# Fused attention and FFN on one core: the reciprocals' small transfers go from SyncE to ScalarE, the scheduler's prices for the partial sums are changed, and the whole order is drawn again

## The chip, the cores and the metric

The kernel runs on one core of one Trainium2 chip. Each core has five engines that run their own instruction streams in order: TensorE (PE; its weight loads are shown as PEld), VectorE (DVE), ScalarE (ACT), GpSimd (POOL) and SyncE (SP, which here issues transfers and computes nothing). An instruction waits at the head of its engine's stream until the semaphores it needs have come. The metric is the device time of the program in microseconds (us), less is better; of several runs the median is compared.

## The reference

```python
# q, k, v: (4, 12, 448, 64) float32; x: (4, 448, 768)
scores = scale * np.matmul(q, k.transpose(0, 1, 3, 2))      # causal mask, softmax over keys
scores = np.where(mask, -1000000000.0, scores)
scores = scores - np.max(scores, axis=-1, keepdims=True)
attn = np.exp(scores)
attn = attn / (np.sum(attn, axis=-1, keepdims=True) + 1e-09)
x = np.matmul(attn, v)                                       # heads side by side: d_model 768
...
mu = np.mean(x, axis=-1, keepdims=True)
var = np.mean((x - mu) ** 2, axis=-1, keepdims=True)
xn = (x - mu) / np.sqrt(var + 1e-06) * g_ln
ch = np.maximum(xn @ w_ch1, 0.0) @ w_ch2                     # 768 -> 3072 -> 768
return (x + ch).astype(np.float32)
```

Four batches, each an attention over twelve heads, then a layer norm and a two-layer network (FFN) with a residual.

## The kernel before

**The work.** The FFN is most of TensorE's stream. Every float32 operand is split into a high and a low part (`xh`, `xl`, `wh`, `wl`, `hh`, `hl`), and a product is three fast matmuls (high by high, high by low, low by high) of 128 x 128 weights and 448 columns. `ph` is a PSUM tile of the first layer (18 matmuls), `po` one of the second (36). These use three PSUM banks, tag `mm`. After a `ph`, ACT writes `hh` and DVE `hl`; after a `po`, DVE adds it to `xT`. The FFN of batches 0 and 1 runs in 96 slots `s` of 18 matmuls; the FFN of batches 2 and 3 runs at the end together (class `Pair`, tiles `bX`, `bY`, `bA`, with weights `wk` and `wp`).

**Attention** of a batch is done in six pairs of heads and is woven into the FFN before it: batch 1 beside batch 0's FFN, batches 2 and 3 beside batch 1's. `STARTS` gives the slot at which each pair is due. Batches 0 to 2 compute scores `sc` with queries on the partitions, exponentials `P`, normalise (`norm`), transpose on TensorE (`pt`) and multiply by `v` (`px`).

**Batch 3 has transposed scores** (`crossed`, `most`, `added`, `crossed_pv`): keys on the partitions, so nothing is transposed, but maximum and sum go across partitions. For each pair of heads:

1. TensorE writes the scores into two banks a head, one of tag `sc` and one of tag `pt` (two of each tag, so the next pair's scores need this pair's banks back).
2. DVE adds the mask (`bars`) and folds the blocks into `most`; POOL's `partition_all_reduce` gives the maximum `all`; DVE subtracts it (`P<-sc,all`, four instructions a head, the last readers of the banks); ACT takes the exponentials.
3. `added`: `sum` is made of one copy and three DVE additions of unequal width a head, POOL sums it over the partitions, and the row goes to DRAM (`turn`, one transfer a head), comes back as 64 x 14 (`r14`, shown as `r<-turn`), DVE adds 1e-9 and takes the reciprocal, it goes to DRAM again (`turnb<-r`) and comes back broadcast over 64 partitions (`over<-turnb`, one a head). Six small transfers a pair, 36 in all, all issued by SP, in line with all other loads and stores.
4. `crossed_pv`: TensorE multiplies `P` by `v` into `px` (a bank of tag `pv`, of which there is one), and DVE writes `xT = px * over`. A pair of heads that stands in `TWOT` is done with its neighbour: both `px` in a row, the second into a bank of tag `pt`.

After the sixth pair the mean `mb` is a matmul over the sum `acc` of the six `xT` (high and low part, `acch` and `accl`), then squares `xc`, the variance `var`, and its spread `rb`, which the inputs of `Pair` need (`xg`, and from them `xh`, `xl`, `xT1h`, `xT2h` and others).

**What sets the order.** The kernel records all instructions, and a scheduler in plain Python (`Plan.schedule`, `Plan.run`) orders them with a cost for each (`Plan.cost`: time on the engine, delay until others see the result, whether it shares a port), due times, and PSUM and SBUF buffers. The costs are in ns and are the planner's own, not measurements. `MOVES` shifts the due times of instructions picked by a pseudo-random draw: each entry has a seed, a size, a share, and a stretch. So any change of a cost, a slot or a seed gives another order on all engines.

Of the kernel before, what the change touches and what calls it, by code (L numbers as in the profile page):

```python
# [20 lines left out]
B, H, S, D = 4, 12, 448, 64  # L21
# [17 lines left out]
HOLE = [-7, 5]  # L39
EARLY = 44  # L40
GAP = 5
SECOND = 32000
BEHIND = 8400
EARLY_SLOT = 1450
SLACK, DMA_SLACK = 192, 5280
# [1 line left out]
IDLE, SLOWED = 2200, 4500  # L47
PASSES, PORT, LEAST, AFTER, URGENT, START = 6, 300, 300, 1500, 5000, 70000
MOVES = [
# [4 lines left out]
]  # L54
STEPS = 6
FIRST = -19
RAT0, TAT0, NAT0, END0, EV0 = [-2, 1, 3], [7, 8, 9, 10, 11], [6, 6], 13, [1, 1, 0, 1, 0]
BOTH, RAT = {1: [0, 1, 2, 3], 2: [5], 3: []}, [1, 0, 0]
SAT, TAT, NAT, END = [1, 0, 1, 0, 2], [4, 5, 5, 6, 6], [3, 3], 8
EV1, EV = [1, 1, 1, 1, 1], [1, 1, 0, 1, 0]  # L60
STARTS = {
    0: [-1, 6, 12, 17, 24, 30],
    1: [0, 5, 10, 14, 19, 24],
    2: [28, 32, 35, 39, 42, 46],
    3: [58, 61, 65, 68, 72, 75],
}
SPREAD1 = 43
PAIR = 84
KEEP0 = 36
TWOS = {}  # L70
VAR0, RB0, XC, XG = 1, 5, 3, 3
SPLIT, SENT, WIDE = (1, 2, 3), (), ('mb',)
COPIED = [6, 6, 4, 0]
AHEAD0 = 4
WARM, FILL, HOLD = 10, 29160, 3200
LATE = {"PR": 3500, "full": 6000, "qkraw": 6000, "vt": 3000, "kept": 2500, "scratch": 1500}
LEFT = {1: (0, 0), 2: (0, 1), 3: "S4", 4: (1, 1), 5: "S1", 6: "S2", 7: "S3"}
RIGHT = {1: "B11", 2: "B21", 3: "B22", 4: "T4", 5: "T1", 6: "T2", 7: "T3"}
ORDER1, ORDER2 = [1, 2, 6, 5, 7, 3, 4], [1, 5, 6, 3, 7, 2, 4]
KB, GX = KC // 2, 2  # L80
ELAG = [1, 4, 9]
BANKS = [("sc", 2), ("sc", 2), ("pt", 2), ("pt", 2), ("pv", 1), ("mm", 3), ("mm", 3), ("mm", 3)]
TURNED, OFFPOOL, LIBRARY, LAZY = {2: [], 3: [0, 1, 2, 3, 4, 5]}, (2, 3), 6300, 12000
KEYS = [(0, 0, 448), (128, 128, 320), (256, 256, 192), (320, 384, 64)]
SCT, SUMT, ENDT = 0, 4, 6
PB, VB, TWOT = 3, 1, {3: [0, 2, 4]}
NORMS = ['PPPPPP', 'EPPPPP', 'EEEEEE', 'EEEEEE']
NTMP, AHEAD = 6, 6
LAST = 239 / 256

# [115 lines left out]
class Plan:  # L206
# [99 lines left out]
    def cost(self, t):  # L306
        n, sbuf = t.size, [x for x in t.ins if x.buf.pool.space is None and x.idx.size > 8]
        psum = any(x.buf.pool.space == PSUM for x in t.ins)
        t.here = 0
        if t.engine == "sync":  # L310
            x = (t.outs + t.ins)[0]
            rate = 100 if n == P else 360 if x.p[1] - x.p[0] == P else 240 if x.p[1] - x.p[0] == D else 150 if n == 512 else 330
            cost = 650 if x.buf.name == "first_qk" else 60
            if x.buf.name.startswith("row"):
                return 60, 8000 * 320, False
            if any(y.buf.name.startswith("turn") for y in t.outs + t.ins):
                return 60, (500 if n < S else 100 if x.p[1] - x.p[0] == 1 else 640) * 320, False
            return cost, (x.p[1] - x.p[0]) * n * 4 * 320 / rate, False
        if t.engine == "tensor":
            if t.kw.get("rhs") is not None and t.kw["rhs"].dtype == BF16:  # L320
                return 0.84 * n, 220, False
            if t.method == "transpose":
                t.mode = "turned"
                return 97 if t.ins[0].dtype == F32 else 78, 220, False
            if t.kw["rhs"].dtype == F32R:
                return max(0.4175 * n + 2, 112), 220, False
            wide = t.outs[0].p[1] - t.outs[0].p[0] > D and t.kw["rhs"].p[1] - t.kw["rhs"].p[0] > D
            t.mode = "" if wide else "rows" if t.outs[0].p[1] > D + t.outs[0].p[0] else "columns"
            return (1.68 if wide else 0.84) * n + 5 if n > 1 else 195, 220, False
        if t.engine == "scalar":  # L330
            t.here = 100
            if t.kw.get("func") == ACTF.Exp:
                t.here = 10
                return 0.84 * n + 277, 70, False
            if isinstance(t.kw.get("scale"), View):
                return 0.835 * n + 188, 160, False
            more = 50 if not psum and t.ins[0].idx.flat[1] > t.ins[0].idx.flat[0] + 1 else 0
            return 0.835 * n + more + (66 if psum else 155 if "scale" in t.kw else 94), 160, False
        if t.engine == "gpsimd":
            t.here = 30  # L340
            if t.method == "memset":
                return 95 + 0.84 * n, 90, False
            if t.method == "tensor_scalar":
                return 240 + 0.835 * n, 90, True
            if t.method == "partition_all_reduce":
                t.mode = "library"
                return (1730 if t.kw["reduce_op"] == bass_isa.ReduceOp.max else 2970), 90, False
            return 2.5 * n + 60 if n > 8 else 1500, 90, bool(sbuf)
        t.here = 85
        if t.method == "bn_stats":  # L350
            n = t.ins[0].idx.size
        tiny = t.method == "tensor_scalar_add" and not psum and t.outs[0].buf.name != "r"
        fast = t.method in ("tensor_copy", "tensor_scalar") and not psum and n > 8
        more = 130 if n <= 8 or t.method == "tensor_scalar" and fast else 75
        if "accum_out" in t.kw:
            t.here = 150
        if n <= 8 and t.method in ("tensor_scalar_add", "reciprocal"):
            more = 68 if t.method == "tensor_scalar_add" else 96
        if t.method == "scalar_tensor_tensor" and isinstance(t.kw["scalar"], View):
            more = 128  # L360
        if t.method == "tensor_tensor" and t.outs[0].p[0]:
            more = 187
        return n / (1.92 if fast else 0.96) + more, t.here + 60, fast or tiny or (len(sbuf) > 1 and not psum)

    def schedule(self):
# [267 lines left out]
def kernel(ctx, tc, qk, v, w1, w2, g, out):  # L633
    nc = plan = Plan()
# [171 lines left out]
    class Att:  # L806
# [204 lines left out]
        def added(self, p):  # L1011
            V = nc.vector
            row = dr.tile([1, 2 * S], F32, name=f"turn{self.b}{p}")
            back = dr.tile([1, 2 * S], F32, name=f"turnb{self.b}{p}")
            for h in range(2):
# [5 lines left out]
                V.tensor_tensor(out=z[:, 3 * P:], in0=z[:, 3 * P:], in1=e[:, :D], op=ALU.add)  # L1021
                t = ap.tile([P, S], F32, tag="PT", name="all", bufs=8)
                nc.gpsimd.partition_all_reduce(t, z, channels=P, reduce_op=bass_isa.ReduceOp.add)
                nc.sync.dma_start(out=row[:, S * h:S * h + S], in_=t[:1, :])
            r = ap.tile([P, S], F32, tag="PT", name="r14", bufs=8)[:D, :14]
            flat = lambda t: t.rearrange("o (p x) -> (o p) x", p=D)
            nc.sync.dma_start(out=r, in_=row.turned(flat))
            V.tensor_scalar_add(r, r, 1e-9)
            V.reciprocal(r, r)
            nc.sync.dma_start(out=back.turned(flat), in_=r)  # L1030
            t = ap.tile([P, S], F32, tag=("y", "rb")[p % 2], name="over", bufs=1)
            for h in range(2):
                nc.sync.dma_start(
                    out=t[D * h:D * h + D, :], in_=back[:, S * h:S * h + S].turned(lambda t: t.broadcast_to([D, S])),
                )
            self.t["over", p] = t
# [835 lines left out]
```

## Time and profile before

| | before |
|---|---|
| median of 3 runs | 807.77 us (807.57 to 810.73) |
| profiled execution, its own time | 806.13 us |
| its span, first to last instruction | 804.2 us |
| TensorE busy | 782.8 us, 97% of the span |
| VectorE busy | 670.9 us, 83% |
| ScalarE busy | 488.0 us, 61% |
| GpSimd busy | 350.8 us, 44% |

The profile shows one execution. Busy time is an average over stages; what a change is worth is read from the stretch in which TensorE stands idle and from what ended the idle time. In a timeline row the bracket at the end is the idle time ahead of the row and what ended it.

### The profile page before, as it was taken

The numbers are of one execution on the slowest core, as the hardware profiler recorded it, in microseconds if no ns is written. First come the engines' busy times: TensorE is split into PE (matmuls) and PEld (weight loads), VectorE is DVE, ScalarE is ACT, GpSimd is POOL, SyncE is SP. The second block draws the span as 40 slices with busy tenths as digits, with TensorE's granted clock in tenths as the row PEclk, the third lists the DMA queues.
The fourth block names the chain that finished last, engine by engine and source line by source line (L and its number), as shares of the span: only waits on it lengthen the run. The fifth ranks groups of instructions, "written<-read, shape, count | busy, mean of one in ns | idle before, by whom it ended". The sixth has DMA issues, their size and how long they took to land. (4 is left out here: it accounts for less than half of the span.)

```text
span 804.2 us, 13502 instructions
## 1 busy us (share of the span) xinstructions
PE 782.8 (97%) x4434; PEld 711.8 (88%) x4434; DVE 670.9 (83%) x1396; ACT 488.0 (61%) x1046; POOL 350.8 (44%) x346
## 2 busy tenths in 40 slices
PE   9999999999999999998989799899999999999998
PEld 4679887898999878987969599899999999999997
DVE  6899987789989985899989659598888878878785
ACT  7999987889999963441343234574555546455461
POOL 4742024344162350255554018755545454464540
PEclk9999999999999999999999899999999999999999
DMA  9778897878888787754472687135244342533424
GB/s 230 266 245 298 311 330 271 303 270 276 286 288 306 235 255 247 255 167 130 135 224 79 226 304 243 56 111 164 74 126 139 88 149 63 158 99 112 123 90 167
DMA packets 69630, 158.80 MB, mean 197 GB/s; under 512 B 14989, under 2 KB 37785, under 8 KB 69561
## 3 DMA queue, kind: packets, MB, share of 16 engines
q1 hardware_dynamic: 69560, 157.95, 59.5%
q8 instruction: 35, 0.57, 0.3%
q14 instruction: 35, 0.28, 0.1%
HBM read 115.92 MB, written 39.99 MB: 194 GB/s over the span
## 5 line engine op out<-in xcount | busy, mean ns | idle before, releaser
L624 PE MATMUL ph<-xh,wh 128*128 128x450 f32 (+1 forms) x288 | 103.1, 363 | 2.2 <-ACT wh L624 2.1
L624 PE MATMUL ph<-xh,wl 128*128 128x450 f32 (+1 forms) x288 | 103.5, 364 | 0.0
L624 PE MATMUL po<-hh,wl 128*128 128x448 f32 x288 | 102.5, 360 | 0.0
L624 PE MATMUL po<-hl,wh 128*128 128x448 f32 x288 | 101.9, 359 | 0.0
L624 PE MATMUL po<-hh,wh 128*128 128x448 f32 x288 | 101.3, 358 | 0.0
L624 PE MATMUL ph<-xl,wh 128*128 128x450 f32 (+1 forms) x288 | 101.2, 357 | 0.0
L624 ACT ACTIVATE wp<-s 128x256 fp32r<-128x256 f32 (+1 forms) x114 | 51.6, 462 | 60.3 <-PE bY L624 15.9
L624 POOL TENSOR_TENSOR s<-u 128x256 f32<-128x256 f32 (+1 forms) x60 | 55.3, 939 | 64.4 <-DMA u<-scratch 50.3
L624 POOL TENSOR_SCALAR P<-P,r 112x336 f32<-112x336 f32 (+3 forms) x72 | 47.0, 671 | 64.6 <-DVE r L624 64.3
L624 ACT ACTIVATE wk<-u 128x256 fp32r<-128x256 f32 (+1 forms) x89 | 41.4, 466 | 52.5 <-PE bX L624 34.1
L624 ACT ACTIVATE P<-P,least 112x224 f32<-112x224 f32 (+3 forms) x128 | 67.2, 535 | 9.4 <-DVE least L624 9.4
L624 DVE TENSOR_TENSOR wp<-s,wp 128x256 fp32r<-128x256 f32 (+1 forms) x120 | 67.9, 577 | 1.6 <-ACT wp L624 1.2
L624 POOL TENSOR_TENSOR h<-b,h 128x448 fp32r<-128x448 f32 x36 | 43.4, 1207 | 53.5 <-ACT h L624 26.8
L624 DVE CUSTOM_DVE_ANT_0 P<-sc,mask 112x448 f32<-112x448 f32 (+3 forms) x128 | 51.9, 443 | 13.6 <-PE sc L624 12.0
L624 PEld LDWEIGHTS ph<-xh,wh 128*128 128x128 f32 x288 | 55.0, 191 | 4.3 <-ACT wh L624 2.6
L624 PEld LDWEIGHTS ph<-xh,wl 128*128 128x128 f32 x288 | 54.9, 191 | 2.5 <-issue 1.4
L624 PEld LDWEIGHTS po<-hh,wh 128*128 128x128 f32 x288 | 54.4, 189 | 2.1 <-issue 1.6
L624 PEld LDWEIGHTS po<-hl,wh 128*128 128x128 f32 x288 | 54.2, 189 | 2.1 <-issue 1.4
L624 PEld LDWEIGHTS ph<-xl,wh 128*128 128x128 f32 x288 | 55.0, 191 | 1.1 <-issue 0.7
L624 DVE TENSOR_TENSOR xT<-xT,bX 128x448 f32<-128x448 f32 (+1 forms) x73 | 44.6, 613 | 13.2 <-PE bX L624 13.1
L624 PEld LDWEIGHTS po<-hh,wl 128*128 128x128 f32 x288 | 54.3, 189 | 0.9 <-issue 0.5
L624 DVE TENSOR_TENSOR wl<-w,wh 128x768 fp32r<-128x768 f32 x48 | 48.8, 1018 | 3.1 <-ACT wh L624 2.8
(211 smaller groups left out, 2142.4 us busy)
## 6 DMA issues: line engine op xcount, KB each, us to landing
raw<-w_dram SPq DMA_DIRECT2D x39, 768.0 KB, 6.5
scratch<-w SPq DMA_DIRECT2D x48, 384.0 KB, 7.2
full<-scratch SPq DMA_DIRECT2D x24, 768.0 KB, 4.9
kept<-wl SPq DMA_DIRECT2D x30, 384.0 KB, 3.1
u<-scratch SPq DMA_DIRECT2D x24, 384.0 KB, 3.7
u<-scratch SPq DMA_DIRECT2D x36, 256.0 KB, 3.0
rawx<-w_dram SPq DMA_DIRECT2D x9, 768.0 KB
wk<-kept SPq DMA_DIRECT2D x36, 192.0 KB, 2.8
```

Source lines behind the costliest of these rows:

```text
L624: getattr(getattr(nc, t.engine), method)(*args, **kw)
```

## The change

Three things change together. The 36 small transfers of `added` are issued by ScalarE (`nc.scalar.dma_start`) instead of SyncE. The planner gets costs for such transfers, and higher ones for the partial sums (`sum`, by a factor on the width) and for the reciprocals' two small instructions. And a set of numbers is redrawn: eleven entries of `MOVES` in place of seven, batch 3 two slots earlier (`STARTS`), `px` one slot nearer to the sums (`ENDT`), `TWOT` with one group in place of three, one pair of batch 1 computed with split operands instead of float32 (`BOTH`), no copies `PR` for batch 2 (`COPIED`, so 40 transposes read float32), more buffers for the squares (`XC`), and a few more.

```diff
-SECOND = 32000
+SECOND = 40000
...
 MOVES = [
-    (350531306, 20000, 16, 222682, 242682), (643024262, 300, 16, 431899, 491899),
...
+    (1073045041, 20000, 128, 329116, 389116), (318057034, 8000, 256, 508939, 568939),
...
-BOTH, RAT = {1: [0, 1, 2, 3], 2: [5], 3: []}, [1, 0, 0]
+BOTH, RAT = {1: [0, 1, 2], 2: [5], 3: []}, [1, 0, 0]
...
-    3: [58, 61, 65, 68, 72, 75],
+    3: [56, 59, 63, 66, 70, 73],
...
-VAR0, RB0, XC, XG = 1, 5, 3, 3
+VAR0, RB0, XC, XG = 1, 5, 5, 3
...
-COPIED = [6, 6, 4, 0]
-AHEAD0 = 4
+COPIED = [6, 6, 6, 0]
+AHEAD0 = 3
...
-TURNED, OFFPOOL, LIBRARY, LAZY = {2: [], 3: [0, 1, 2, 3, 4, 5]}, (2, 3), 6300, 12000
+TURNED, OFFPOOL, LIBRARY, LAZY = {2: [], 3: [0, 1, 2, 3, 4, 5]}, (2, 3), 6300, 16800
...
-SCT, SUMT, ENDT = 0, 4, 6
-PB, VB, TWOT = 3, 1, {3: [0, 2, 4]}
-NORMS = ['PPPPPP', 'EPPPPP', 'EEEEEE', 'EEEEEE']
+SCT, SUMT, ENDT = 0, 4, 5
+PB, VB, TWOT = 3, 1, {3: [4]}
+NORMS = ['PPPPPP', 'EPPPPP', 'EEEEPA', 'EEEEEE']
...
+        if t.method == "dma_start" and t.engine == "scalar":
+            t.here = 3000 if n == S and t.outs[0].p[1] > D - 1 + t.outs[0].p[0] else 2200
+            return 70, t.here, False
...
+        if t.outs[0].buf.name == "sum" and t.method == "tensor_tensor":
+            return 1.8 * n + 180, t.here + 60, True
+        if t.outs[0].buf.name == "r14":
+            more = 480 if t.method == "tensor_scalar_add" else 200
...
-                nc.sync.dma_start(out=row[:, S * h:S * h + S], in_=t[:1, :])
+                nc.scalar.dma_start(out=row[:, S * h:S * h + S], in_=t[:1, :])
...
-            nc.sync.dma_start(out=r, in_=row.turned(flat))
+            nc.scalar.dma_start(out=r, in_=row.turned(flat))
             V.tensor_scalar_add(r, r, 1e-9)
             V.reciprocal(r, r)
-            nc.sync.dma_start(out=back.turned(flat), in_=r)
+            nc.scalar.dma_start(out=back.turned(flat), in_=r)
...
             for h in range(2):
-                nc.sync.dma_start(
+                nc.scalar.dma_start(
                     out=t[D * h:D * h + D, :], in_=back[:, S * h:S * h + S].turned(lambda t: t.broadcast_to([D, S])),
                 )
```

**First place: TensorE, the end of batch 3's attention.** In the rows of the order the number in front is the row's place on that engine; a run of equal instructions is one row. Before, the mean `mb` and the spread `rb` of batch 2 stand one FFN matmul behind the last two `px`:

```order
1831 L624 MATMUL px<-P,vt 64x192
1832 L624 MATMUL px<-P,vt 64x64 x3
1833 L624 MATMUL ph<-xh,wl 128x448
1834 L624 MATMUL rb<-ident,ve 128x112 x4
1835 L624 MATMUL mb<-acch,ones 128x448
1836 L624 MATMUL mb<-accl,ones 128x448
1837 L624 MATMUL ph<-xh,wh 128x448
```

Now the last `px` ends at row 1798, the mean comes at 1877 behind 78 FFN matmuls, and that `rb` at 1909:

```order
1797 L633 MATMUL px<-P,vt 64x192
1798 L633 MATMUL px<-P,vt 64x64 x3
1799 L633 MATMUL ph<-xh,wh 128x448
...
1876 L633 MATMUL ph<-xh,wl 128x448
1877 L633 MATMUL mb<-acch,ones 128x448
1878 L633 MATMUL mb<-accl,ones 128x448
1879 L633 MATMUL ph<-xh,wh 128x448
```

Between the sixth pair's last scores and the mean 120 FFN matmuls stood before, and 148 stand there now.

**Second place: TensorE, the first two `px` of batch 3.** Before, the products of pairs 0 and 1 stand together (the first four rows into `pv`, the next four into a bank of tag `pt`), behind the third pair's scores:

```order
1506 L624 MATMUL po<-hl,wh 128x448
1507 L624 MATMUL px<-P,vt 64x448 x2
1508 L624 MATMUL px<-P,vt 64x320 x2
1509 L624 MATMUL px<-P,vt 64x192 x2
1510 L624 MATMUL px<-P,vt 64x64 x2
1511 L624 MATMUL px<-P,vt 64x448 x2
1512 L624 MATMUL px<-P,vt 64x320 x2
1513 L624 MATMUL px<-P,vt 64x192 x2
1514 L624 MATMUL px<-P,vt 64x64 x2
1515 L624 MATMUL po<-hh,wl 128x448
```

Now pair 0's product stands alone, right behind the second pair's scores; pair 1's comes alone too, at rows 1582 to 1585, seven FFN matmuls ahead of the fourth pair's scores:

```order
1472 L633 MATMUL sc<-qkraw 128x448 x2
1473 L633 MATMUL sc<-qkraw 128x64 x2
1474 L633 MATMUL sc<-qkraw 128x320 x2
1475 L633 MATMUL sc<-qkraw 128x192 x2
1476 L633 MATMUL px<-P,vt 64x448 x2
1477 L633 MATMUL px<-P,vt 64x320 x2
1478 L633 MATMUL px<-P,vt 64x192 x2
1479 L633 MATMUL px<-P,vt 64x64 x2
1480 L633 MATMUL po<-hl,wh 128x448
```

What moved: four of the six products of batch 3 no longer come in twos, and only the last two use a `pt` bank.

**Third place: the last pair's small transfers.** Before, on SP, among the loads of `v` and the stores of weight parts (`turn_5149`, `r_5202` and `turnb_5228` are the last pair's; `turnb_5113` is the pair's before it):

```order
274 L624 DMA turn_5149<-all 1x448
275 L624 DMA vt<-v_dram 48x2x64
276 L624 DMA vt<-v_dram 16x2x64
277 L624 DMA over<-turnb_5113 64x448
278 L624 DMA r_5202<-turn_5149 64x14
279 L624 DMA vt<-v_dram 112x2x64
280 L624 DMA over<-turnb_5113 64x448
281 L624 DMA vt<-v_dram 16x2x64
282 L624 DMA turnb_5228<-r_5202 64x14
283 L624 DMA full<-scratch_2446 128x1536
284 L624 DMA over<-turnb_5228 64x448 x2
```

Now, on ACT, among the evacuations `hh` of the FFN's first layer (`turn_5182`, `r_5240` and `turnb_5273` are the last pair's; `r_5173` and `turnb_5227` the pair's before it):

```order
494 L633 ACTIVATE hh<-ph 128x448
495 L633 DMA r_5173<-turn_5132 64x14
496 L633 DMA turn_5182<-all 1x448 x2
497 L633 DMA turnb_5227<-r_5173 64x14
498 L633 DMA r_5240<-turn_5182 64x14
499 L633 ACTIVATE hh<-ph 128x448
500 L633 DMA over<-turnb_5227 64x448 x2
501 L633 DMA turnb_5273<-r_5240 64x14
502 L633 ACTIVATE hh<-ph 128x448
503 L633 DMA over<-turnb_5273 64x448 x2
504 L633 ACTIVATE hh<-ph 128x448
```

What moved: three `hh` evacuations, rows 499, 502 and 504, now stand behind transfers that wait for GpSimd's sums or for an earlier transfer's landing.

## Rows read from the trace of the kernel before

**Rows 1.** The profile's page, part 1: busy us, share of the span, instructions.
```profile
PE 782.8 (97%) x4434; PEld 711.8 (88%) x4434; DVE 670.9 (83%) x1396; ACT 488.0 (61%) x1046; POOL 350.8 (44%) x346
```

**Rows 2.** Busy us by stretch (PE, PEld, DVE, ACT, POOL), then TensorE's granted clock, DMA share.
```profile
360.00:455.00 95.00, 86.58 (x493) 75.18 (x493) 81.08 (x170) 25.91 (x48) 44.47 (x19) 0.98 0.49 148
...
440.00:460.00 20.00, 14.56 (x80) 11.62 (x79) 12.56 (x23) 3.94 (x7) 0.77 (x1) 0.88 0.60 200
...
480.00:500.00 20.00, 20.00 (x108) 19.98 (x107) 19.97 (x27) 10.71 (x19) 14.67 (x12) 1.00 0.84 285
```

**Rows 3.** TensorE's timeline: start, us, instruction, in brackets idle before and its releaser.
```profile
242.10 0.26 PE L624 MATMUL pt<-ident,P 112*112 112x112 f32 x1
242.13 0.33 PE L624 MATMUL sc<-kh,qs 128*112 128x224 f32 x1
...
359.88 2.11 PE L624 MATMUL sc<-qkraw 64*128 64x448 f32 x16
...
372.04 5.37 PE L624 MATMUL px<-P,vt 128*64 128x448 f32 x32 [2.67 <-issue]
...
412.19 3.68 PE L624 MATMUL px<-P,vt 128*64 128x448 f32 x32 [0.45 <-DVE P L624]
...
422.57 1.10 PE L624 MATMUL sc<-qkraw 64*128 64x320 f32 x6 [2.00 <-DVE xT L624]
...
453.10 0.57 PE L624 MATMUL rb<-ident,ve 112*128 112x112 f32 x4 [2.68 <-DVE xT L624]
454.10 0.46 PE L624 MATMUL mb<-acch,ones 128*128 128x448 f32 x1 [0.43 <-DVE acch L624]
454.76 0.46 PE L624 MATMUL mb<-accl,ones 128*128 128x448 f32 x1 [0.20 <-DVE accl L624]
457.34 0.74 PE L624 MATMUL ph<-xh,wh 128*128 128x448 f32 x1 [2.13 <-ACT wh L624]
457.88 0.58 PE L624 MATMUL ph<-xl,wh 128*128 128x448 f32 x1
458.25 0.58 PE L624 MATMUL ph<-xh,wh 128*128 128x448 f32 x1
...
514.22 0.46 PE L624 MATMUL bA<-xl,wk 128*128 128x448 f32 x1 [2.39 <-POOL xl L624]
```

**Rows 4.** VectorE's timeline, pairs 2, 4 and 5 of batch 3.
```profile
381.52 1.41 DVE L624 TENSOR_TENSOR P<-sc,all 128x448 f32<-128x448 f32 x4
...
416.15 2.25 DVE L624 TENSOR_TENSOR sum<-sum,P 128x192 f32<-128x192 f32 x2
...
424.40 1.67 DVE L624 TENSOR_TENSOR most<-sc,most 128x320 f32<-128x320 f32 x6
...
430.79 1.41 DVE L624 TENSOR_TENSOR P<-sc,all 128x448 f32<-128x448 f32 x4
...
454.08 0.62 DVE L624 TENSOR_TENSOR accl<-acc,acch 128x448 fp32r<-128x448 f32 x1
```

**Rows 5.** GpSimd's timeline, the last sum over the partitions.
```profile
437.90 2.87 POOL L624 PARTITION_ALL_REDUCE all<-sum  x1 [1.52 <-DVE sum L624]
```

**Rows 6.** SP's timeline, issues of the last pair's small transfers.
```profile
441.09 1.22 SPq L624 DMA_DIRECT2D vt<-v_dram  x2
...
443.04 0.54 SPq L624 DMA_DIRECT2D r<-turn  x1
...
445.91 0.47 SPq L624 DMA_DIRECT2D turnb<-r  x1
...
447.78 1.08 SPq L624 DMA_DIRECT2D over<-turnb  x2
```

**Rows 7.** TensorE's groups by form: count, busy us, mean ns.
```profile
L624 PE MATMUL pt<-ident,P 112*112 112x112 f32 x280 | 42.0, 263 | 2.8 <-ACT PT L624 1.1 <-POOL P L624 1.0 <-DVE PT L624 0.3
...
L624 PE MATMUL pt<-ident,PR 112*112 112x112 f32 x40 | 4.3, 238 | 0.0
```

**Rows 8.** TensorE's timeline, one pair's product alone (batch 2).
```profile
293.70 2.11 PE L624 MATMUL px<-PT,vt 112*64 112x448 f32 x16
```

More of the change, by code (lines that the diff above doesn't have):

```diff
@@ L68 @@
 PAIR = 84
-KEEP0 = 36
+KEEP0 = 37
 TWOS = {}
-VAR0, RB0, XC, XG = 1, 5, 3, 3
+VAR0, RB0, XC, XG = 1, 5, 5, 3
 SPLIT, SENT, WIDE = (1, 2, 3), (), ('mb',)
-COPIED = [6, 6, 4, 0]
-AHEAD0 = 4
+COPIED = [6, 6, 6, 0]
+AHEAD0 = 3
 WARM, FILL, HOLD = 10, 29160, 3200
@@ L80 @@
 KB, GX = KC // 2, 2
-ELAG = [1, 4, 9]
+ELAG = [1, 3, 9]
 BANKS = [("sc", 2), ("sc", 2), ("pt", 2), ("pt", 2), ("pv", 1), ("mm", 3), ("mm", 3), ("mm", 3)]
-TURNED, OFFPOOL, LIBRARY, LAZY = {2: [], 3: [0, 1, 2, 3, 4, 5]}, (2, 3), 6300, 12000
+TURNED, OFFPOOL, LIBRARY, LAZY = {2: [], 3: [0, 1, 2, 3, 4, 5]}, (2, 3), 6300, 16800
 KEYS = [(0, 0, 448), (128, 128, 320), (256, 256, 192), (320, 384, 64)]
-SCT, SUMT, ENDT = 0, 4, 6
-PB, VB, TWOT = 3, 1, {3: [0, 2, 4]}
-NORMS = ['PPPPPP', 'EPPPPP', 'EEEEEE', 'EEEEEE']
+SCT, SUMT, ENDT = 0, 4, 5
+PB, VB, TWOT = 3, 1, {3: [4]}
+NORMS = ['PPPPPP', 'EPPPPP', 'EEEEPA', 'EEEEEE']
 NTMP, AHEAD = 6, 6
```

8 rows, old and new, of the table MOVES are left out of this document.

## The prediction

> **What bounds the kernel now.** I read the page's table of engines first: TensorE is busy for 97% of the span [rows 1], so time can only be won where it stands idle, where its clock is low, or where work leaves it. In a full stretch (480 to 500 us) 107 weight loads fill 19.98 us: one FFN matmul takes 0.187 us [rows 2]. TensorE's timeline then shows where it does not run so. From 360 to 455 us batch 3's pairs are woven in; ScalarE is busy there for only 25.91 of 95 us, VectorE for 81.08 [rows 2]. The idle brackets are 2.67 us ahead of the first double product `px` (372.04), 0.45 and 2.00 at later pairs, then 2.68, 0.43, 0.20 and 2.13 around the mean, and 2.39 ahead of the first `bA` on the pair's inputs (514.22) [rows 3]: 12.95 us.
>
> The clock costs more. After the pause at 372 the 32 matmuls of `px` take 5.37 us, where the same 32 take 3.68 at 412: 1.69 us [rows 3]. After the pauses at 453 to 457 the next matmuls start 0.37 us apart, twice the 0.187; from 440 to 460 the granted clock is 0.88 on average, between the levels of 1.2 and 2.4 GHz, against 1.00 at 480 to 500 [rows 2, 3]. Twelve matmuls at the longer pitch cost 12 x 0.185 = 2.2 us. In all 12.95 + 1.69 + 2.2 = **16.8 us** are lost between 360 and 515. That is what a better order can win; about 4 us of other gaps lie ahead of batch 3, and I leave them.
>
> Why is it idle at 372? The bracket says only that nothing shown released it. The second product of that double `px` goes to a `pt` bank, and the third pair's scores hold it until their subtractions have read it: these end at 382.93 for the second head, 20.9 us after the scores (end 359.88 + 2.11 = 361.99) [rows 3, 4]. For the last pair the same leg is short: scores end 422.57 + 1.10 = 423.67, subtractions 430.79 + 1.41 = 432.20, 8.5 us later.
>
> **The last pair's chain** (one after another): scores end 423.67; subtractions 432.20; GpSimd's sum of the second head 437.90 + 2.87 = 440.77; `r` issued 443.04, `turnb` 445.91, `over` from 447.78; `accl` ready 454.08 + 0.62 = 454.70 [rows 3 to 6]. From scores to mean: 31.0 us, of which the transfers' part (440.77 to 447.78) is 7.0. Two loads of `vt` (1.22 us of SP) stand between `turn` and `r` [rows 6].
>
> **The change, part by part.**
>
> *Transfers on ScalarE.* An issue takes up to 0.54 us (the `r`, and each of two `over` in 1.08) [rows 6]: 36 x 0.54 = 19.5 us at most on an engine with 69 idle us in that stretch. Below nothing it can go by the 1.22 us of `vt` that the last pair no longer stands behind; above, by what waits in line. Row 499 of the order is a `hh` behind `r`. Its transfer can go 17.1 us after the scores for the sum, 0.24 for a wait's end and 2.24 for the landing: 19.6 us, some 20.4 with the issues. TensorE needs that bank about 124 matmuls and the last `px` later: 23.2 + 3.68 = 27 us. About 6 us of cover, so I price it at nothing; if the cover goes, everything behind `hh` waits. The landing legs I keep. The Trainium skill (DMA: Bandwidth & Descriptors, "Issuing engines are not separate DMA queues") says that issuing from a second engine saves only the sequencer's issue time, and that the transfers run on the same 16 engines. By it the legs stay and at most the 1.22 us goes, which would take the mean's wait below from 1.5 to 0.3; the sum by rows is not altered.
>
> *`px` one by one.* The second bank is no longer needed for pairs 0 to 3, so the 2.67 us and the 1.69 of slow clock go: the bank that a lone `px` uses is its own. Price: 16 matmuls alone take 2.11 us [rows 8], half of 3.68 is 1.84: 0.27 x 4 = 1.1 us.
>
> *Next pair's scores.* Between one pair's scores and the next there are now 41 or 42 FFN matmuls and one `px`: 42 x 0.187 + 2.1 = 10.0 us. The banks come free after 8.5 us in the short case. VectorE works nearly all of it, so of the 0.45 + 2.00 us I leave 0.3 (0 to 1; 10.9 more each if the leg is 20.9).
>
> *The mean later.* 148 FFN matmuls and the last double `px` lie between last scores and mean: 27.7 + 3.7 = 31.4 us, for a chain of 31.0. GpSimd now does the last sums behind other sums, and VectorE's sums took 2.25 us for two beside it [rows 4]; I stretch the chain by 0.9 to 2.9 (one sum of 2.87 in its way at most): 31.9 to 33.9, and a wait of 0.5 to 2.5, taken as 1.5. Of 2.68 + 0.43 + 0.20 + 2.13 and 2.2 of slow clock that leaves 1.5.
>
> *Inputs of the last stage.* From `rb` to the first `b` matmul 172 FFN matmuls stood, 144 stand now: 5.2 us less cover. The wait there was 2.39. It could be 2.39 + 5.2 = 7.6 at the worst if the chain behind `rb` was all at work, and nothing if it stood in line behind other work; `xl` is GpSimd's, which is also freed earlier. I take 2.5, nearly what it was (0 to 5).
>
> *Work on TensorE.* Forty transposes read `P` in place of `PR`: 263 against 238 ns [rows 7], at most 40 x 0.025 = 1.0; least 0, if they overlap. The scores and transposes stand in 31 fewer groups; a lone transpose is followed 0.03 us later by the next matmul [rows 3], so 31 x 0.03 = 0.9 back, with the split pair of batch 1 about 1.1 (0 to 2). With `px` 1.1: +1.0 in all.
>
> *The rest of the redrawn order* has no row: every other engine's sequence changes. Least: none. Most: two pauses such as the 2.67 (5 us). I take 1.5.
>
> Sum: left over are 0.3 + 1.5 + 2.5 + 1.0 + 1.5 = 6.8 of 16.8, so 10.0 us come back: 806.13 - 10.0 = 796.1. The profiled run lies 1.64 under the median of 807.77, so **about 798 us**. With the terms' ends (0 + 0.5 + 0 + 0 + 0 and 1 + 2.5 + 5 + 2 + 5, which hardly come together) its own range is 793.5 to 803.
>
> **The rivals.**
>
> *All waits vanish.* The mean's wait goes with the 1.22 us, the input's chain was in line rather than at work, and the rest is nothing: only +1.0 stays of 16.8, and 807.77 - 15.8 = 792. For it: much idle time on ScalarE. Against: VectorE is busy 85% of the stretch.
>
> *VectorE and GpSimd stand in each other's way.* GpSimd now alternates maxima and sums in pairs and does four sums in a row at the end; each addition `sum` of VectorE that meets one can wait up to its 2.87 us. Two or three such in the last pair make the mean wait 5.7 more than the 1.5; TensorE then pauses, and its clock falls for the 2.2 us seen at 457 (less 1.1 of the rest): 798 + 5.7 + 2.2 - 1.1 = 804.8. For it: 81 of 95 us, and 2.25 us for two additions. The Trainium skill (SBUF — State Buffer, "SBUF: two separate sides") says that the port pair of the two engines is an exclusive lock, held for a whole instruction, against two-input operations of VectorE where GpSimd reads SBUF. The row of 2.25 us at 416.15 does not decide whether an addition waited; by that page it can.
>
> *Slower: the last pair is as late as pair 2 was.* If something ahead of the last pair's subtractions holds VectorE as it did then (20.9 instead of 8.5 us), the chain is 12.4 us longer, all of it is seen by TensorE at the mean, and the clock falls (1.69 or 2.2, and again behind the second pause: 3.4 in all). 798 + 12.4 + 3.4 - 0.4 = 813.4. ScalarE's line of `hh` behind `r`, past its 6 us of cover, is one way to this. It ends above before's median once the chain is some 7 us late (7 + 3.0 of clock against 9.8). Against: pair 5's leg was short already.
>
> *It changes nothing*: the new order loses elsewhere what it wins, near 807.
>
> **How the numbers follow.** Likeliest 0.50 (798); all vanish 0.14 (792); the two engines in each other's way 0.20 (804.8); slower 0.12 (813.4); nothing 0.04. A difference of 0.5% (4.0 us) is about what a measurement of this kernel can tell from no change: faster is under 803.7, slower over 811.8. Faster: 0.14 + 0.47 + 0.05 = 0.66; same: 0.03 + 0.13 + 0.04 = 0.20; slower: 0.02 + 0.12 = 0.14. The range reaches from the lower case to half of what is above 804.8: 791 to 809.
>
> **What the profile after would show.** Right: no pause and full pitch at the first `px`; `px` alone at about 2.1 us; under 1 us of idle ahead of the later pairs' scores; 0.5 to 2.5 us at `mb`, and no matmuls 0.37 us apart behind it; 0 to 5 us ahead of the first of the last stage. ScalarE's transfers issued in under 0.6 us each, and no `ph` that waits for `hh`. Wrong: a pause of over 4 us anywhere with a low clock behind it, additions over 2 us each, subtractions that end more than 15 us after their scores, or TensorE's busy time up by over 3 us.

## The result and the profile after

The changed kernel takes 798.87 us (median of 4 runs, 797.73 to 803.4), the kernel before 807.67 (4 runs, 807.37 to 810.73) beside it: ratio 0.9893, 95% interval 0.9848 to 0.9938. The profiled execution took 797.73 us, its span 795.9 against 804.2. The forecast was 798. That it was met so closely is partly luck, as the parts below show: the pauses that stayed and the work on TensorE were both wrong by several us, in opposite directions. The four executions of the changed kernel had a mean granted clock of 0.998, 0.994, 0.998 and 0.991; the profiled one is the fastest of them.

The page of the changed kernel, part 1, to be held against [rows 1]:

```profile
PE 776.9 (98%) x4434; PEld 713.5 (90%) x4434; DVE 669.9 (84%) x1378; ACT 493.8 (62%) x1056; POOL 363.3 (46%) x359
```

TensorE is busy 5.9 us less with the same number of instructions. VectorE has no less to do. The windows answer to [rows 2] (busy us of PE, PEld, DVE, ACT, POOL, then granted clock, DMA share, GB/s):

```profile
360.00:455.00 95.00, 85.19 (x490) 76.57 (x488) 82.68 (x179) 35.61 (x65) 47.55 (x21) 1.00 0.56 179
440.00:460.00 20.00, 16.64 (x79) 15.71 (x78) 13.38 (x26) 4.53 (x9) 0.00 (x0) 0.91 0.76 255
```

ScalarE has taken on 10 us there, and still stands idle for 59 of 95. TensorE is idle there for 9.8 us, before for 8.4; its clock is higher (1.00 for 0.98). TensorE's timeline, which answers to [rows 3]:

```profile
369.69 2.11 PE L633 MATMUL sc<-qkraw 64*128 64x448 f32 x16 [0.29 <-DVE P L633]
...
380.05 1.95 PE L633 MATMUL px<-P,vt 128*64 128x448 f32 x16 [1.63 <-issue]
...
395.88 1.95 PE L633 MATMUL px<-P,vt 128*64 128x448 f32 x16 [1.26 <-issue]
...
411.68 1.95 PE L633 MATMUL px<-P,vt 128*64 128x448 f32 x16 [1.58 <-ACT hh L633]
...
429.85 0.46 PE L633 MATMUL ph<-xh,wl 128*128 128x448 f32 x1 [1.90 <-DVE wl L633]
...
454.92 0.46 PE L633 MATMUL mb<-acch,ones 128*128 128x448 f32 x1 [3.16 <-DVE acch L633]
455.58 0.74 PE L633 MATMUL mb<-accl,ones 128*128 128x448 f32 x1 [0.20 <-DVE accl L633]
456.11 0.58 PE L633 MATMUL ph<-xh,wh 128*128 128x448 f32 x1
456.48 0.58 PE L633 MATMUL ph<-xl,wh 128*128 128x448 f32 x1
...
524.60 0.46 PE L633 MATMUL bY<-xB22h,wp 128*128 128x448 f32 x1 [1.01 <-DVE bY L633]
```

The one pause of 2.67 us ahead of the double `px` has become three shorter ones, 4.47 us together, ahead of lone `px`. No clock is lost behind them: each `px` takes 1.95 us, and FFN matmuls go on 0.19 us apart. Behind the 3.16 us at the mean the matmuls start 0.37 us apart again, seven of them.

Where the 8.3 us of the span came from. "Work" is the sum of the distances from one matmul's start to the next over the whole trace, less the pauses, so it holds what the clock costs.

| us | before | after | difference |
|---|---|---|---|
| pauses from 360 us to the first inputs of the last stage | 12.95 | 0.29 + 1.63 + 1.26 + 1.58 + 1.90 + 3.16 + 0.20 + 1.01 = 11.03 | -1.9 |
| all other pauses | 3.90 | 3.46 | -0.4 |
| slow clock | 1.69 + 2.2 = 3.9 | 7 x 0.185 = 1.3 | -2.6 |
| work at full clock | 782.46 - 3.9 = 778.6 | 776.58 - 1.3 = 775.3 | -3.3 |

By kind, the work before and after is 343.57 and 340.29 for `ph` and `po`, 51.00 and 48.24 for `px`, 33.37 and 34.48 for `pt`, 55.38 and 55.12 for `sc`; the last stage (`bX`, `bA`, `bY`) takes 0.7 us less. Of the first two differences 0.9 and 1.69 us are clock.

The 2.6 us of clock belong to these two executions. Experiment 2 below keeps the order of before and pauses as long at the same place, 2.76 us for 2.67, and its 32 matmuls of `px` take 3.68 us at full clock, for 5.37:

```profile
372.70 3.68 PE L627 MATMUL px<-P,vt 128*64 128x448 f32 x32 [2.76 <-issue]
```

### The profile page after: what moved, and what is told of

The parts are those of the page before. It is cut to its first block, busy times and chain, and to the rows that moved or that the text cites. A ratio compares the mean times of both kernels' runs of the same rounds, so it can differ in the third digit from the quotient of the medians.

```text
span 795.9 us, 13484 instructions
## 1 busy us (share of the span) xinstructions
PE 776.9 (98%) x4434; PEld 713.5 (90%) x4434; DVE 669.9 (84%) x1378; ACT 493.8 (62%) x1056; POOL 363.3 (46%) x359
## 4 chain that ended last, share of the span: by engine, by line
PE 82%; DVE 7%; DMA 5%; ACT 3%; issue 2%; ACTq 0%; DVEq 0%; POOL 0%; SPq 0%; POOLq 0%
PE bX L633 20%; PE po L633 17%; PE ph L633 16%; PE bY L633 10%; PE bA L633 5%; PE px L633 4%; PE sc L633 4%; PE pt L633 4%; DVE wl L633 2%; DMA turnb<-r 2%; DMA over<-turnb 2%; ACT P L633 2%; DMA r<-turn 1%; DVE P L633 1%; ACT rest L633 1%
## 5 line engine op out<-in xcount | busy, mean ns | idle before, releaser
L633 ACT ACTIVATE wp<-s 128x256 fp32r<-128x256 f32 (+1 forms) x113 | 51.2, 462 | 59.7 <-PE bX L633 20.6
L633 POOL TENSOR_SCALAR P<-P,r 112x112 f32<-112x112 f32 (+3 forms) x82 | 53.8, 676 | 56.7 <-DVE r L633 46.4
L633 ACT ACTIVATE P<-P,least 112x112 f32<-112x112 f32 (+3 forms) x128 | 66.7, 526 | 11.1 <-DVE least L633 10.7
L633 DVE TENSOR_TENSOR wp<-s,wp 128x256 fp32r<-128x256 f32 (+1 forms) x120 | 71.4, 603 | 1.4 <-ACT wp L633 0.9
L633 ACT ACTIVATE wk<-u 128x256 fp32r<-128x256 f32 (+1 forms) x89 | 41.1, 464 | 48.1 <-PE bX L633 34.2
L633 DVE CUSTOM_DVE_ANT_0 P<-sc,mask 112x224 f32<-112x224 f32 (+3 forms) x128 | 52.2, 442 | 11.1 <-PE sc L633 9.0
L633 DVE TENSOR_TENSOR wl<-w,wh 128x768 fp32r<-128x768 f32 x48 | 53.5, 1114 | 4.8 <-ACT wh L633 4.5
```

The costliest lines, as they stand in the source:

```text
L633: getattr(getattr(nc, t.engine), method)(*args, **kw)
```

## The experiments

The scheduler makes one list of all instructions, and each engine takes its own from it in that order. So a queue can be changed with the order kept, by naming another engine when the list is issued. Eight of the twelve experiments take such a list and change the queue, a few places or one kind of instruction in it.

**1. The changed order, transfers on SP.**

```diff
-                getattr(getattr(nc, t.engine), method)(*args, **kw)
+                engine = "sync" if method == "dma_start" and t.engine == "scalar" else t.engine
+                getattr(getattr(nc, engine), method)(*args, **kw)
```

> The changed kernel with its order kept on every engine, and the 36 small transfers issued by SP at their places in that order. Theory 1 (the redrawn order gives the gain, the queue is worth nothing by itself): 797 to 801 us. Theory 2 (the queue gives the gain, since on SP a waiting transfer holds back all loads behind it): SP waits for each row, weights and values come late, new pauses of 1 us and more ahead of weight parts, 802 to 808 us. Theory 3 (on ScalarE the small transfers run beside large loads, which on SP would have waited behind them, and so land later): the last pair's time from turnb to over goes back from 5.0 to about 2 us and the wait at the mean from 3.2 to under 1 us, whatever the total does.

799.32 us (797.69 to 800.33), ratio to before 0.9902 (0.9886 to 0.9917): all of the gain is there without ScalarE. Its pauses come to 14.5 us, as in the changed kernel, but in other places. The time from the last pair's `turnb` to `over` stayed long, 4.4 us, and the wait at the mean grew, so theory 3 as put there fell. SP's and TensorE's timelines:

```profile
446.09 0.46 SPq L634 DMA_DIRECT2D turnb<-r  x1
450.47 1.09 SPq L634 DMA_DIRECT2D over<-turnb  x2
```

```profile
456.88 0.74 PE L634 MATMUL mb<-acch,ones 128*128 128x448 f32 x1 [4.20 <-DVE acch L634]
```

The Trainium skill (DMA: Bandwidth & Descriptors, "Issuing engines are not separate DMA queues") says that issuing from another engine saves only issue time; the times of these two kernels agree, 799.32 against 798.87.

**2. The order of before, transfers on ScalarE.** The same edit the other way about.

> The kernel before with its order kept on every engine, and the 36 small transfers issued by ScalarE at their places in that order. Theory 1 (order): 806 to 809 us, as before. Theory 2 (queue): the 9 to 17 us between turnb and over of pairs 0 to 4 fall to about 3 us, but the products that wait there are placed late anyway; gain of 1 to 4 us, 803 to 806. Theory 3 (load): the last pair's time from turnb to over grows from 1.9 to 3 to 5 us, and the wait ahead of the mean by as much: 808 to 811 us.

808.63 us (10 runs, 806.43 to 812.75) beside 807.17, ratio 1.0024 (1.0008 to 1.0041). The queue alone gives nothing; by the interval it costs 0.1 to 0.4%. From `turnb` to `over` pairs 0 to 4 still took 8 to 18 us: the `over` are placed late in that order, and no queue moves them. The last pair's leg stayed short on ScalarE, 1.67 us (449.55 to 451.22), so theory 3 fell here too, though the time lies in its range as well as in theory 1's.

**3. The old numbers with the new queue and its price in the planner**, so that another order comes out.

```diff
+        if t.method == "dma_start" and t.engine == "scalar":
+            t.here = 3000 if n == S and t.outs[0].p[1] > D - 1 + t.outs[0].p[0] else 2200
+            return 70, t.here, False
...
-                nc.sync.dma_start(out=row[:, S * h:S * h + S], in_=t[:1, :])
+                nc.scalar.dma_start(out=row[:, S * h:S * h + S], in_=t[:1, :])
```

> The kernel before with the four issuing lines and the planner's price for such transfers, and nothing else: the old numbers give a new order. Theory 1 (the gain is in the redrawn numbers): 804 to 812 us, no better than before. Theory 2 (queue): 798 to 803 us.

818.83 us, ratio 1.0153 (1.0126 to 1.0179): 12 us worse than the order of before, and worse than either theory had it.

**4, 10, 11. Neighbours of the changed order.** In one the seed of the first entry of `MOVES` is 1073045042 for 1073045041, in one that of the ninth is 1886329053 for 1886329052, and in one the prices for `sum` and `r14` are taken out.

> The changed kernel with one seed of one entry of MOVES changed by one: the same queue, prices and due times, another draw of the due times behind 329 us in the plan. Theory 1 (the gain is this draw's): 801 to 808 us. Rival (queue, prices and slots give the gain whatever the draw): 797 to 801 us.

> The changed kernel with the seed of another entry of MOVES changed by one, the one for 394 to 399 us of the plan, 5 us wide. Theory 1 (the gain is this draw's): between 799 and 808 us, a further value. Rival (the first other seed was an unlucky one, and most draws give the gain): 797 to 800 us.

> The changed kernel without the new prices for the partial sums and for the two small instructions of the reciprocals, all other numbers as changed: another order. Theory 1 (a draw is good for the prices it was drawn with): 802 to 812 us. Rival (the prices don't matter for the order): 797 to 800 us.

806.39 us (ratio 0.9994, 0.997 to 1.0018), 807.55 (1.0000, 0.9981 to 1.0019) and 805.93 (0.9982, 0.9971 to 0.9993). Each keeps the queue, the slots, `TWOT` and nearly all numbers of the change, and each is back at the time before. So the gain hangs on this one draw together with its prices. A stall of the first neighbour stands on ScalarE's timeline (the second row's transfers wait for `turnb`):

```profile
370.68 0.48 ACTq L633 DMA_DIRECT2D turnb<-r  x1
...
377.71 1.11 ACTq L633 DMA_DIRECT2D over<-turnb  x2
378.87 0.54 ACT L633 ACTIVATE most<-sc 128x448 f32<-128x448 f32 x1 [5.93 <-issue]
```

and on VectorE's, where the same draw makes it wait:

```profile
379.45 1.68 DVE L633 TENSOR_TENSOR most<-sc,most 128x320 f32<-128x320 f32 x6 [5.08 <-ACT most L633]
```

A `most` stood behind `over` on ScalarE, and VectorE behind that `most`. This is the forecast's line of work behind a waiting transfer, on another instruction than `hh`.

**5. That first neighbour, its order kept, transfers on SP.** The edit of experiment 1.

> The order with one seed changed (806.4 us with transfers on ScalarE), kept on every engine, and the 36 small transfers issued by SP. In that order ScalarE stood 5 us at a transfer `over` while the maxima `most` queued behind it, and VectorE waited 5.08 us for `most`. Theory 4 (what this draw loses, it loses because ScalarE stands behind transfers whose landing is stretched by loads beside them): with SP issuing, ScalarE goes on, VectorE's wait for `most` goes, 799 to 803 us. Rival (the draw loses by its places on TensorE and VectorE, whoever issues): 805 to 809 us.

807.92 us (1.0006, 0.999 to 1.0023). Theory 4 fell: with ScalarE free the draw is no better. A pause of 3.67 us ahead of a `px` and one of 3.12 at the mean stay. The stall on ScalarE is real, and without it the time is no less.

**6. Experiment 1 with three large transfers (`full`, `wl`, `kept`) moved from beside the last pair's `turnb` and `over` to behind them.**

```diff
+        order = plan.schedule()[0]
+        small = [n for n in order if plan.tasks[n].engine == "scalar" and plan.tasks[n].method == "dma_start"]
+        first, last = order.index(small[-4]), order.index(small[-1])
+        loads = [n for n in order[first:last] if plan.tasks[n].engine == "sync"]
+        order = plan.later(order, loads, small[-1])
+        plan.issue(tc.nc, order)
```

> The changed order with all small transfers on SP, as in the first experiment, and the three large transfers that stand between the last pair's turnb and over (a weight load of 768 KB, a load and a store of weight parts) moved behind that over; nothing else moves. Theory 3b (the landing time goes by the load on the DMA engines, not by the issuing queue): from turnb to over 1.7 to 2.2 us instead of 4.4, the wait at the mean shorter by 2 us or more, 796 to 798 us. Rival (the leg is long for another reason): still over 4 us, time unchanged within 1 us.

797.96 us (0.9897, 0.987 to 0.9924), which the intervals do not tell from experiment 1. SP's timeline:

```profile
446.36 0.46 SPq L649 DMA_DIRECT2D turnb<-r  x1
448.56 1.08 SPq L649 DMA_DIRECT2D over<-turnb  x2
449.74 0.53 SPq L649 DMA_DIRECT2D full<-scratch  x1
```

The leg is 2.20 us, where experiment 1 had 4.4. The same leg's window in four kernels (the last two figures of a row are DMA share and GB/s): before, changed, experiment 1, experiment 6.

```profile
445.90:447.80 1.90, 1.90 (x11) 0.85 (x11) 0.00 (x0) 0.00 (x0) 0.00 (x0) 1.00 0.22 56
```

```profile
444.60:449.60 5.00, 5.00 (x28) 5.00 (x27) 1.47 (x3) 0.54 (x1) 0.00 (x0) 1.00 0.94 272
```

```profile
446.10:450.50 4.40, 4.40 (x25) 4.40 (x24) 3.06 (x6) 0.54 (x1) 0.00 (x0) 1.00 0.93 297
```

```profile
446.40:448.60 2.20, 2.20 (x14) 2.20 (x13) 0.99 (x3) 0.00 (x0) 0.00 (x0) 1.00 0.30 82
```

In these four the leg of a transfer of 3.5 KB takes 2 us with the DMA engines a quarter busy and 4.4 to 5 with them full, whoever issued it, and moving the loads away shortened it. The share alone does not set it: pair 1's leg in the changed kernel (384.21 to 387.35) took 3.1 us at a share of 0.79, pair 3's in experiment 12 (417.25 to 421.63) 4.4 at 0.31. TensorE's timeline of this kernel shows what became of the time:

```profile
454.22 0.46 PE L649 MATMUL mb<-acch,ones 128*128 128x448 f32 x1 [0.99 <-DVE acch L649]
...
465.45 1.40 PE L649 MATMUL var<-g_sb,xc 128*112 128x1 f32 x8 [2.53 <-DVE xc L649]
```

The wait at the mean fell from 4.20 us in experiment 1 to 0.99, and 2.53 came back at the variance.

**7, 8. TensorE's places alone.** The lone `px` of pairs 1, 2 and 3 go behind the next 9, 7 and 9 FFN matmuls; in the second kernel `mb` also goes 36 later.

> The changed kernel with three of its lone products px (pairs 1, 2 and 3) moved later on TensorE, behind the next 9, 7 and 9 FFN matmuls; the waits there were 1.63, 1.26 and 1.58 us. Theory 5 (these waits are only places: the bank of tag pv is not free until the pair before has its xT, and ready FFN matmuls stand behind): 4.5 us come back, 794 to 796 us. Rival (the chain of pairs on VectorE and GpSimd sets the end, and the time comes back as longer waits at later scores and at the mean): 797 to 800 us.

> As the one with px moved, and the mean mb moved behind 36 more FFN matmuls (6.8 us), where it waited 3.16 us. Theory 5: with 4.5 us at px, 3.4 at the mean and 1.3 of slow clock, 789 to 793 us. Rival (chain): the wait moves to the variance, the spread and the inputs of the last stage: 796 to 800 us.

806.55 us (0.9992, 0.997 to 1.0014) and 806.06 (0.9989, 0.9963 to 1.0014): the whole gain is lost. Both theories had the wrong size, and the rival the right direction. TensorE's timeline of the first:

```profile
382.85 5.31 PE L648 MATMUL sc<-qkraw 64*128 64x320 f32 x16 [3.50 <-DVE P L648]
389.13 3.68 PE L648 MATMUL px<-P,vt 128*64 128x448 f32 x16
...
463.66 0.74 PE L648 MATMUL mb<-acch,ones 128*128 128x448 f32 x1 [8.25 <-DVE acch L648]
```

Pair 3's scores wait for their bank until VectorE has done pair 2's subtractions. In the changed kernel TensorE waits 1.63 us and does the `px` before that moment; here it waits 3.50 us in one piece, the scores take 5.31 us at the low clock instead of 2.27 and the next `px` 3.68 instead of 1.95, and VectorE gets everything that much later, down to 8.25 us at the mean. In the second kernel those 8 us stand at the variance (8.36).

**9. No sums on GpSimd.** The twelve sums over the partitions become a memset of their output.

```diff
+                if method == "partition_all_reduce" and kw["reduce_op"] == bass_isa.ReduceOp.add:
+                    method, args, kw = "memset", [args[0], 1.0], {}
```

> The changed kernel, order kept, with GpSimd's twelve sums over the partitions of batch 3 replaced by a memset of their output: the sums are left out, the rest stands. Theory 6 (the chain of batch 3's pairs on VectorE and GpSimd sets the waits of TensorE, and GpSimd's 2.9 us sums are in it twice: by themselves, and by the two-input instructions of VectorE that stand still beside them, 15.8 us in all): the waits at px (4.5 us) and at the mean (3.4 us, 1.3 of slow clock) go, VectorE is busy some 16 us less; 788 to 792 us. Rival (the waits hang on the landing of the small transfers or on TensorE's places): over 795 us.

797.21 us (794.68 to 799.51; 0.9871, 0.9844 to 0.9897), hardly better than the changed kernel. The page, part 1:

```profile
PE 780.0 (98%) x4434; PEld 714.4 (90%) x4434; DVE 655.2 (82%) x1378; ACT 493.7 (62%) x1056; POOL 331.7 (42%) x359
```

GpSimd is free of 31.6 us and VectorE of 14.7, and by the medians 1.7 us of that reached the time: theory 6's 788 to 792 falls. The rival named there, the landing of small transfers, took the sums' place. The three pauses ahead of lone `px` became one, with the low clock behind it (TensorE's timeline):

```profile
383.01 3.68 PE L635 MATMUL px<-P,vt 128*64 128x448 f32 x16 [4.23 <-issue]
```

It begins at pair 0's `r`, which took 5.9 us from its issue (366.54) until VectorE could use it, where the changed kernel took 2.4 (367.80 to 370.23); why is open. Then a `most` stood behind `over` on ScalarE, VectorE waited 2.72 us for it, and pair 0's `xT`, which the `px` needs, came late. VectorE's and ScalarE's timelines:

```profile
372.48 0.17 DVE L635 TENSOR_SCALAR r<-r 64x14 f32<-64x14 f32 x1 [3.57 <-DMA r<-turn]
```

```profile
377.93 0.54 ACT L635 ACTIVATE most<-sc 128x448 f32<-128x448 f32 x1 [3.82 <-issue]
```

At the last pair ScalarE's timeline shows this:

```profile
433.17 0.84 ACT L635 ACTIVATE wh<-full 128x768 fp32r<-128x768 f32 x1 [1.90 <-PE ph L635]
...
434.00 0.70 ACTq L635 DMA_DIRECT2D turn<-all  x2
```

The last pair's rows were there at 427.5, and its `turn` went out at 434.0, in its place in ScalarE's line behind a `wh` that waited for TensorE; in the changed kernel they went at 434.7 and 437.9. From the second of them to `over` it took 14.3 us here and 11.8 there (DMA share 0.82 to 0.92 here), and the mean waited 3.00 us for 3.16.

**12. The last pair's transfers on SP with the loads behind them, all others on ScalarE**, as a version that might beat both kernels.

> The changed kernel and its order, with the transfers of pairs 0 to 4 on ScalarE as they are, and those of the last pair alone on SP, with the three large transfers that stood beside its turnb and over moved behind them. Theory 3b and the sixth run together: from turnb to over about 2.2 us instead of 5.0, the waits at px as in the changed kernel (1.3 to 1.7 us, on SP one of them was 4 us and more), the wait at the mean under 1.5 us: 2 us less than the changed kernel, 796 to 797.5 us. Rival (the next link gives it back, as the variance's wait of 2.53 us did in the sixth run): 798 to 800 us.

798.36 us (5 runs, 797.32 to 798.77; 0.9884, 0.9867 to 0.9901): no different from the changed kernel. The leg from `turnb` to `over` is 2.57 us, the mean does not wait at all, and the rival holds:

```profile
464.33 1.15 PE L649 MATMUL var<-g_sb,xc 128*112 128x1 f32 x8 [3.02 <-DVE xc L649]
```

## Why the prediction was right, and where it was not

**Transfers on ScalarE, priced at nothing: right.** Experiments 1 and 2 show it from both sides. No `ph` waited for `hh`.

**`px` one by one.** The step "the bank that a lone `px` uses is its own" failed. There is one bank of tag `pv`, and the next `px` can't start before VectorE has written the pair before to `xT`: those ended at 379.8, 395.7 and 411.5, and the `px` start at 380.05, 395.88 and 411.68, each 0.21 us later. VectorE's timeline:

```profile
379.23 0.61 DVE L633 TENSOR_TENSOR xT<-px,over 128x448 f32<-128x448 f32 x1
...
395.04 0.62 DVE L633 TENSOR_TENSOR xT<-px,over 128x448 f32<-128x448 f32 x1 [2.27 <-DMA over<-turnb]
...
410.86 0.61 DVE L633 TENSOR_TENSOR xT<-px,over 128x448 f32<-128x448 f32 x1
```

The second of them waited for its `over` to land. The brackets of the `px` name `issue` and a `hh` that had ended at 411.0. The forecast had 0 there; it was 4.47 us. The 1.69 us of clock came back as forecast, but experiment 2 had them back with the pause still there, so it is not shown that the shorter pauses gave them. The price of a lone `px` was taken from batch 2, 2.11 us; batch 3's takes 1.95, so 0.11 x 4 = 0.4 us and not 1.1.

The pause at 372 was read rightly as a wait for a `pt` bank, but from the wrong row. The subtractions that end at 382.93 are the second head's and come after the `px` were done (377.41). The bank was the first head's, whose subtractions are this row of VectorE's timeline before:

```profile
371.26 1.34 DVE L624 TENSOR_TENSOR P<-sc,all 128x320 f32<-128x320 f32 x4
```

The second of the four is the last reader of that bank; it ended at 371.94, 0.10 us ahead of the `px`, and 0.10 ahead in experiment 2 as well. So the leg that held the bank was 9.9 us, not 20.9.

**Next scores: right**, 0.29 us for 0.3.

**The mean: mis-sized.** Forecast was a wait of 1.5; measured were 3.16 + 0.20 and 1.3 of slow clock. The chain from the last scores' end (415.27 + 2.27 = 417.54) to `accl` (455.52) took 38.0 us, for 31.9 to 33.9. The changed kernel's rows for it, of GpSimd, ScalarE and VectorE:

```profile
431.53 6.32 POOL L633 PARTITION_ALL_REDUCE all<-sum  x2 [1.62 <-DVE sum L633]
```

```profile
434.71 3.37 ACTq L633 DMA_DIRECT2D turn<-all  x2
440.26 0.47 ACTq L633 DMA_DIRECT2D turnb<-r  x1
440.85 0.54 ACTq L633 DMA_DIRECT2D r<-turn  x1
...
444.60 0.55 ACTq L633 DMA_DIRECT2D turnb<-r  x1
...
449.64 1.15 ACTq L633 DMA_DIRECT2D over<-turnb  x2
```

```profile
454.89 0.63 DVE L633 TENSOR_TENSOR accl<-acc,acch 128x448 fp32r<-128x448 f32 x1
```

The last sum ends at 437.85, 20.3 us after the scores for 17.1 in [rows 5]: 3.2 us more, just over the 0.9 to 2.9 allowed. From there to `over` it is 11.8 us, where [rows 6] had 7.0; of the 4.8 us more, 3.2 are the leg from `turnb` to `over`. The wait did not grow by as much as the chain, because TensorE came to the mean 34.2 us after the scores for 31.4, 1.90 of that by the pause at 429.85. The step that failed is "the landing legs I keep": the redrawn order put large loads beside the last pair's transfers, where before there were small pieces of `vt` and one `full` (DMA share 0.22), and experiment 6 shows, with SP issuing, that this is the cause for the leg to `over`.

**Inputs of the last stage: mis-sized**, 1.01 us for 2.5.

**Work on TensorE: wrong sign**, 3.3 us less for 1.0 more. The step that failed is "31 x 0.03 = 0.9 back". It priced only the transpose, and the matmul behind a group pays too. TensorE's timeline of the changed kernel:

```profile
235.91 0.55 PE L633 MATMUL pt<-ident,P 112*112 112x112 f32 x4
236.23 0.44 PE L633 MATMUL po<-hh,wl 128*128 128x448 f32 x1
236.50 0.35 PE L633 MATMUL po<-hh,wh 128*128 128x448 f32 x1
236.69 0.35 PE L633 MATMUL po<-hl,wh 128*128 128x448 f32 x1
```

The first `po` behind the transposes takes 0.27 us until the next starts, the one after it 0.19. There are 20 groups of transposes fewer, and 11 fewer of them stand directly ahead of a `ph` or `po` (53 for 64): 11 x 0.08 = 0.9 us. The `ph` and `po` directly behind scores went from 64 to 55, and what they take over 0.19 us each fell by 1.3 us in all. The `px` that are no longer cut up have their share. The forty transposes cost what was taken at most: `pt` went up by 1.1. That fewer groups are the whole of the 3.3 us was not tested by a run.

**The rest of the order, 1.5**: 1.90 us at 429.85, on `wl` behind VectorE.

In all the forecast left 0.3 + 1.5 + 2.5 + 1.5 = 5.8 us of pauses and slow clock in this stretch where 11.03 + 1.3 = 12.3 stayed, 6.5 too few, and had 4.3 too much work; with 0.4 of other pauses that is the 1.8 us between the 10.0 forecast and the 8.2 of the table. The mechanism that it leaned on most, pauses that vanish, gave 1.9 us. The clock gave 2.6 in these two executions, and the work fell by 3.3 us where the forecast had it rise. So the mechanism was right in part, and that the number was met is luck in good part. Its own range of 793.5 to 803 is narrower than its terms: left over 0.5 to 15.5 of 16.8 us, they give 791.5 to 806.5.

**The rivals.** VectorE does stand still beside GpSimd's sums, but without the sums experiment 9 is by its median only 1.7 us faster, and its wait at the mean is 3.00 us for 3.16. Of the signs named for being wrong two came: an addition of 2.04 us (`sum` at 370.98), and subtractions too late. Of those for being right these failed: the wait at the mean was above 2.5 us, with matmuls 0.37 us apart behind it, and two `over` took 1.33 us to issue (387.35). Subtractions over 15 us after their scores were named as a sign that the forecast was wrong; pair 3's ended 15.8 us after, and it did no harm, since the next scores start only 15.6 us after its own and did not wait. "It changes nothing" was put at 0.04; with three neighbours of the draw at 806 to 808 us a change that redraws the order deserved more.

What stays open is why just this draw is 7 to 9 us better than its neighbours. Their traces show more and longer pauses (23.2 us in experiment 4, 20.6 in 10, 18.5 in 11, for 14.5), in other places each, and the mean granted clock of these profiled executions was 0.996, 0.991 and 0.992 for 0.998. The slots, `TWOT`, `BOTH`, `COPIED` and `XC` were not varied one by one, so what each gave is not known.

## What to carry to other kernels

When a change moves code and redraws an order at once, run each with the other held, and run neighbours of the draw: here one line of issue was worth nothing, and a seed that differs by one was worth the whole gain. A pause in a chain that several engines share was not removed here by moving the instruction that shows it; it turned up at the next link, and worse in experiment 7, where a short pause became a long one with a low clock behind it. A small transfer on a chain landed sooner away from large loads, not on another queue; even that moved a wait and won no time.

## What the runs showed of the hardware

**Clock and pauses.** In the changed kernel the granted clock was full behind pauses of 1.63, 1.26, 1.58 and 1.90 us; behind 2.67 (before), 3.16, 3.50 (experiment 7) and 3.87 us (experiment 1) the matmuls ran at the lower of the two levels, and 16 matmuls of `px` took 3.68 us for 1.95. The length of a pause does not decide it alone. Behind 2.76 us (experiment 2), 3.12 (experiment 5, at the mean) and the 3.06 of this row of experiment 4 the clock was full, and behind one of 2.28 us in experiment 12 (ended at 429.75) it was 0.50 from 430.8 to 434.2:

```profile
382.20 1.95 PE L633 MATMUL px<-P,vt 128*64 128x448 f32 x16 [3.06 <-DMA over<-turnb]
```

**VectorE beside GpSimd's sum.** An addition with two inputs in SBUF that meets a sum over the partitions waits, but not to its end. Changed kernel, GpSimd (two sums in one row) and VectorE:

```profile
385.31 5.73 POOL L633 PARTITION_ALL_REDUCE all<-sum  x2 [4.54 <-ACT wh L633]
```

```profile
385.59 1.75 DVE L633 TENSOR_TENSOR sum<-sum,P 128x64 f32<-128x64 f32 x1
```

The addition usually takes 0.21 us. It ends at 387.34, 2.03 us after the sum's start and some 0.8 before its end (385.31 + 2.87; a profile's spans on GpSimd are rough, but two sums in a row took 5.73). An addition that met the sum at 402.30 gives the same hold: it started at 402.81 and took 1.80 us for 0.48, so 402.81 + 1.80 - 0.48 - 402.30 = 1.83. The Trainium skill (SBUF — State Buffer, "SBUF: two separate sides") says that the lock on the shared ports is held for a whole instruction; in these rows VectorE is held for 1.8 of 2.87 us, and the measurement decides.
